# Row 128 of the sine weights: from 32 matmuls to small DMAs and a sum on VectorE

## The chip, the cores and the metric

The kernel runs on one core of a Trainium2 chip, as one program. The metric is the device time of one execution in microseconds; the median of several runs counts. The engines are named as in the profile: PE is TensorE's matmul, DVE is VectorE, ACT is ScalarE, POOL is GpSimd, and SP is SyncE, which here only issues DMAs. Each engine works through its own queue in order.

## The reference

The input is x of shape (4, 3072, 256). The kernel computes the real part of a two-dimensional discrete Fourier transform of each of the four batches, puts it through a leaky feed-forward layer, and that through a gated one with a token shift:

```python
X = np.fft.fft(np.fft.fft(x, axis=1), axis=2).real          # (4, 3072, 256)
h = X.reshape(-1, 256) @ w_in                               # (12288, 2048)
y = np.maximum(0.01 * h, h) @ w_out                         # (12288, 256)
xk = mu_k * y + (1 - mu_k) * y_prev                         # y_prev: the token before
xr = mu_r * y + (1 - mu_r) * y_prev
out = sigmoid(xr @ w_r) * (np.maximum(xk @ w_k, 0) ** 2 @ w_v)
```

## The kernel before

The transform along the sequence runs on TensorE with tables. The transform along the 256 channels is folded into the first layer's weights: a table of cosines (`cet`) and one of sines (`sot`) are multiplied with w_in once, and what comes out are cosine weights (`weh`, `wel`) and sine weights (`woh`, `wol`), each 128 rows by 2048 columns. The letters h and l stand for a high and a low part: all products are made of three matmuls, high by high, high by low and low by high. The cosine weights would have a row 128 as well, for the frequency in the middle of the 256 channels. It has no place among 128 partitions, and since the sine row of frequency 0 is zero, the values of that row are kept in row 0 of the sine weights, on partition 0.

The first layer works on tiles of 512 tokens (and their 512 mirror images). A tile has 16 units u, each of 128 of the 2048 hidden columns. For each unit `mm_a` multiplies the cosine weights, `ev_a` makes a copy of the result on DVE, and `mm_b` adds the product with the sine weights onto the same PSUM tile; `step` orders this for a unit x and the unit nx after it, and `stage_out` multiplies by w_out two units later. In `ev_a` the row's values come in: there `w128[:, u:u+1]` is a scalar per partition, so the row has to lie along the partitions, 128 values to a column of `w128`. So far `w_in_row` turned it with matmuls: 128 columns of `woh` and `wol` as weights, and a column of two numbers, (1, 0, 0, ...), as the moving operand; ACT copies what comes out into `w128`.

The weights are made while the first tile runs, in eight chunks q of 256 columns, two units each. The steps of a chunk are: `w_in_load` (SP loads 512 KB of 64-bit numbers into a buffer `st`), `w_in_parts` (ACT, DVE and POOL turn them into two 32-bit parts, f and r), `w_in_mm` (matmuls with the tables, L411 for f and L413 for r), `w_in_split` (ACT writes the high part, DVE the low part at L421) and `w_in_row`. Chunks 0 and 1 are done ahead of the loop, the others in `boot(u)`, which runs after each step of the first tile. The weights w_out go a similar way (`w_out_load`, L169 for `uol`). A load waits until its buffer is free, and the buffers are freed by POOL's multiply at L151. SP's queue is one list in program order: an issue that waits holds up those behind it. `load_c` puts one row of the sequence transform on all partitions (`cb`), for `ev_a`.

Of the kernel before, what the change touches and what calls it, by code (L numbers as in the profile page):

```python
# [78 lines left out]
def fft_mlp_kernel(ctx, tc, xs, x7, x8, x87, tb, tbs, alt, ce, so, mu, w_in, w_out, w_k, w_v, w_r, out):  # L79
# [24 lines left out]
    def act_copy(o, i):  # L104
        A.activation(o, i, ACTF.Copy)  # L105
# [277 lines left out]
    V.memset(one0[0:1].bitcast(F32), 1.0)  # L383
    V.memset(c87, 0.0)

    win, wout, wps = {}, {}, {}

    mut = misc.tile([P, 4], F32, name="mut")
    omu = misc.tile([P, 4], F32, name="omu")

    def w_in_load(q, ahead=False):
        if q < 8:
# [28 lines left out]
        V.tensor_tensor(wl2[:, :, sl], o, wh2[:, :, sl].bitcast(F32), op=ALU.subtract)  # L421


    def w_in_row(q):
        if q >= 8:
            return
        ps = win.pop(q)[0]
        for i in range(2):
            f = slice((2 * q + i) * P, (2 * q + i + 1) * P)
            o = ps[:, 2 * i:2 + 2 * i]  # L430
            T.matmul(o, woh[:, f], one0, start=True, stop=False)
            T.matmul(o, wol[:, f], one0, start=False, stop=True)
        act_copy(w128[:, 2 * q:2 * q + 2], ps[:, 0:4].rearrange("p (i t) -> p i t", t=2)[:, :, 0])

    def w_out_load(q, ahead=False):
        if q < 8:
            st = load_f64(w_out[q * 256:(q + 1) * 256].rearrange("(k p) d -> p k d", p=P), 2, D, ahead)
            s = slice(2 * q % HF, 2 * q % HF + 2)
            wout[q] = f64_hi_lo(uoh[2 * q // HF][:, s], uol[2 * q // HF][:, s], st, 2, D, *((mv, "gl") if q < 1 else (stage, "f")))
# [20 lines left out]
    def c_a(src, t0, extra):  # L460
        ps = ps_s.tile([P, 512], F32, tag="s", name="cps")
        c_mm(ps, src, t0, 0, not extra)
        if extra:
            T.matmul(ps[:4, :JP], c87[0:2], altt[0:2].bitcast(F32), start=False, stop=True)
        ev = fft.tile([4, JP], F32, tag="x7", bufs=1, name="cev") if extra else work.tile([4, JP], F32, tag="fv", bufs=2, name="cev")
        act_copy(ev, ps[:4, :JP])
        return ps, ev
# [60 lines left out]
    fold_odd(2, x0[2])  # L528
    w_in_split(1)
    w_out_load(0)  # L530
    ca = c_a(c8m, "c", False)
    c8s = c_fold()
    fold7()
    w_in_row(0)
    cs0 = c_b(c8m, "d", "o", *ca, "g")
    cur_c = load_c(0, 0)
    w_out_load(1, True)
# [2 lines left out]
    w_in_load(3)  # L540
    w_out_load(2)
    Q.dma_start(x87t, x87)
    w_in_row(1)
    po = fft_a(0, "Po")
    qo = fft_a(0, "Qo")
    for g in range(3, 6):
# [13 lines left out]
    def boot(u):  # L560
        q = u // 2
        if u == 0:
            w_in_mm(2, (1,), (0,))
            three0()
            tail0((1,))
            wout[0][1]()
            w_in_load(4)
        elif u % 2 == 0:
            w_in_row(q + 1)
            w_in_mm(q + 2)  # L570
            if q < 8:
                wout[q][0]()
            w_in_load(q + 4)
        else:
            if q == 0:
                w_in_mm(2, (1,), (1,))
            w_in_split(q + 2)
            wout[q][2]()
            w_in_parts(q + 3)
            w_out_load(q + 3)  # L580

    def mm_a(x):
# [6 lines left out]

    def ev_a(x):  # L590
        u = x["u"]
        x["ev"] = work.tile([P, W], F32, tag="as", bufs=2, name="ev")
        V.scalar_tensor_tensor(x["ev"], x["cb"], w128[:, u:u + 1], x["ps"], op0=ALU.mult, op1=ALU.add)  # L593

# [231 lines left out]
    for b in range(B):  # L826
# [4 lines left out]
        for ti in range(NT):  # L831
# [3 lines left out]
            for u in range(NF):  # L835
# [76 lines left out]
                    w2_steps.pop(0)()  # L912
                if b == B - 1:
                    if i == 33:
                        Q.dma_start(mut, mu)
                    if i == 36:
                        V.tensor_scalar(omu, mut, -1.0, 1.0, op0=ALU.mult, op1=ALU.add)
                        loaded[0] = load_tile(0)
                    if i == 39:
                        todo = do_prep(0)  # L920
                    if i in (40, 42, 44, 46):
                        todo.pop(0)()
# [219 lines left out]
```

## Time and profile before

| | us |
|---|---|
| median of three runs | 1490.4 (1489.12 to 1490.57) |
| profiled execution | 1488.97 |
| its span, first to last instruction | 1487.2 |
| PE busy | 1471.9 (99% of the span) |
| DVE, ACT, POOL busy | 1027.1, 893.2, 145.5 |

The granted TensorE clock is 1.000 over the span. A timeline row reads: start, duration, engine, line, operation, output<-inputs, shape; in brackets stands the idle time of the engine before it and what ended it. Lines are those of the kernel before; a line can be that of a helper, as L105 and L112 of the splits into high and low part.

### The profile page before, as it was taken

Reading aid. Unit: us, or ns where it says so; the run is one execution under the profiler, and the core shown is the slowest. Engines: PE = TensorE matmul, PEld = TensorE weight load, DVE = VectorE, ACT = ScalarE, POOL = GpSimd, SP = SyncE. Lnnn points to the kernel's source line nnn. Section 1 sums busy time; section 2 is a strip of 40 time slices with the busy share of each in tenths; the row PEclk is TensorE's granted clock in tenths of the full one; section 3 lists DMA queues with packets and bytes.
Section 4 is the critical chain, followed back from the end, with each engine's and each line's share of the span. In section 5 each row is a group of like instructions: output and inputs, shape, how many; then the busy total and the mean of one; then the engine's idle time right before and its main releaser. Section 6 shows DMA issues by size and latency. Waiting matters only on the chain.

```text
span 1487.2 us, 17785 instructions
## 1 busy us (share of the span) xinstructions
PE 1471.9 (99%) x6520; PEld 1209.9 (81%) x6520; DVE 1027.1 (69%) x1444; ACT 893.2 (60%) x1481; POOL 145.5 (10%) x154
## 2 busy tenths in 40 slices
PE   7999999999999999999999999999999999999998
PEld 4787888888888888888888887888888888888887
DVE  7886766766666766676767666676766666666675
ACT  5576566556666565665666656556565555555564
POOL 2444201131010221010000000000000000000000
PEclk9999999999999999999999999999999999999999
DMA  8646423564032653142220103121212212121200
GB/s 322 192 140 140 88 82 125 174 123 90 15 127 91 198 113 61 36 157 76 95 79 0 57 1 106 65 85 48 80 57 72 68 60 70 58 71 57 72 29 29
DMA packets 86396, 134.24 MB, mean 90 GB/s; under 512 B 29283, under 2 KB 49525, under 8 KB 82724
## 3 DMA queue, kind: packets, MB, share of 16 engines
q1 hardware_dynamic: 70916, 86.49, 17.9%
q0 software_dynamic: 15392, 46.61, 12.4%
q8 instruction: 51, 0.84, 0.2%
q14 instruction: 37, 0.30, 0.1%
HBM read 105.20 MB, written 27.88 MB: 89 GB/s over the span
## 4 chain that ended last, share of the span: by engine, by line
PE 91%; ACT 0%; DVE 0%; POOL 0%; DMA 0%; issue 0%; ACTq 0%; DVEq 0%
PE o L611 33%; PE v L982 17%; PE kps L939 17%; PE ps L600 8%; PE ps L588 8%; PE rps L990 4%; PE dps L632 0%; PE f2Qe L302 0%; PE f1Qe L302 0%; DMA y<-yo 0%; PE f3Qe L302 0%; PE f2Pe L302 0%; PE f1Pe L302 0%; PE f3Pe L302 0%; PE f3Po L302 0%; PE f2Qo L302 0%
## 5 line engine op out<-in xcount | busy, mean ns | idle before, releaser
L677 DVE SCALAR_TENSOR_TENSOR g<-ev,ps 128x512 f32<-128x512 f32 x192 | 131.7, 686 | 182.4 <-PE ps L600 182.4
L943 ACT ACTIVATE rl<-kps 128x512 f32<-128x512 f32 x190 | 113.7, 598 | 230.7 <-PE kps L939 227.2
L659 DVE TENSOR_TENSOR gl<-g,gh 128x1024 fp32r<-128x1024 f32 x192 | 237.8, 1239 | 1.4 <-ACT gh L105 1.4
L944 DVE SCALAR_TENSOR_TENSOR k<-kps,rl 128x512 f32<-128x512 f32 x190 | 131.5, 692 | 148.6 <-ACT rl L943 147.8
L105 ACT ACTIVATE gh<-g 128x1024 fp32r<-128x1024 f32 x192 | 202.7, 1056 | 49.4 <-PE o L611 47.9
L611 PE MATMUL o<-gh,uol 128*128 128x512 f32 x768 | 211.3, 389 | 0.5 <-DVE uol L169 0.5
L611 PE MATMUL o<-gh,uoh 128*128 128x512 f32 x768 | 211.3, 389 | 0.0
L611 PE MATMUL o<-gl,uoh 128*128 128x512 f32 x768 | 211.1, 389 | 0.0
L108 ACT ACTIVATE g<-ps 128x512 f32<-128x512 f32 x192 | 114.5, 596 | 152.4 <-DVE g L677 151.2
L611 PEld LDWEIGHTS o<-gh,uol 128*128 128x128 f32 x768 | 144.0, 188 | 30.9 <-DVE uol L169 1.1
L611 PEld LDWEIGHTS o<-gh,uoh 128*128 128x128 f32 x768 | 144.2, 188 | 30.5
L611 PEld LDWEIGHTS o<-gl,uoh 128*128 128x128 f32 x768 | 144.2, 188 | 30.0
L593 DVE SCALAR_TENSOR_TENSOR ev<-cb,w,ps 128x512 f32<-128x512 f32 x192 | 143.3, 747 | 1.9
L112 DVE TENSOR_TENSOR k2l<-k,k2h 128x512 fp32r<-128x512 f32 x190 | 129.7, 683 | 0.5 <-ACT k2h L105 0.5
L982 PE MATMUL v<-k2h,wvh 128*128 128x512 f32 x382 | 121.6, 389 | 0.1
L982 PE MATMUL v<-k2l,wvh 128*128 128x512 f32 x382 | 121.5, 389 | 0.0
L982 PE MATMUL v<-k2h,wvl 128*128 128x512 f32 x382 | 121.5, 389 | 0.0
L108 ACT ACTIVATE g<-g 128x512 f32<-128x512 f32 x192 | 119.9, 624 | 0.0
L939 PE MATMUL kps<-mh,wkh 128*128 128x512 f32 x380 | 117.2, 390 | 1.5 <-ACT mh L105 0.8
L105 ACT ACTIVATE k2h<-k 128x512 fp32r<-128x512 f32 x190 | 118.4, 623 | 0.0
L939 PE MATMUL kps<-ml,wkh 128*128 128x512 f32 x380 | 117.2, 390 | 0.1
L939 PE MATMUL kps<-mh,wkl 128*128 128x512 f32 x380 | 117.1, 389 | 0.0
(409 smaller groups left out, 2248.5 us busy)
## 6 DMA issues: line engine op xcount, KB each, us to landing
y<-yo SPq DMA_DIRECT2D x24, 512.0 KB
xa<-y SPq DMA_DIRECT2D x24, 512.0 KB
out_dram<-o SPq DMA_DIRECT2D x23, 512.0 KB
tab_a<-in_tbs POOLq DMA_DIRECT2D x8, 1158.0 KB, 6.3
tab_b<-in_tbs POOLq DMA_DIRECT2D x8, 1158.0 KB, 5.4
tab_c<-in_tbs POOLq DMA_DIRECT2D x6, 1158.0 KB, 5.4
tab_d<-in_tbs POOLq DMA_DIRECT2D x6, 1158.0 KB, 5.4
pm<-in_xs POOLq DMA_DIRECT2D x54, 128.0 KB, 3.5
```

What stands on the lines that cost most here:

```text
L105: A.activation(o, i, ACTF.Copy)
L108: A.activation(o, i, ACTF.Prelu, alpha=0.01)
L112: V.tensor_tensor(lo, src, hi.bitcast(F32), op=ALU.subtract)
L588: T.matmul(x["ps"], l[:, f], r, start=(i == 0), stop=(i == 2))
L593: V.scalar_tensor_tensor(x["ev"], x["cb"], w128[:, u:u + 1], x["ps"], op0=ALU.mult, op1=ALU.add)
L600: T.matmul(x["ps"], l[:, f], r, start=False, stop=(i == 2), skip_group_check=True)
L611: T.matmul(po[s][h], w[:, u % HF, h * P:(h + 1) * P], g[:, s], start=(u == 0 and i == 0), stop=(u == NF - 1 and i == 2))
L659: V.tensor_tensor(gl, x["g"], x["gh"].bitcast(F32), op=ALU.subtract)
L677: V.scalar_tensor_tensor(g[:, 1], x["ev"], 2.0, x["ps"], op0=ALU.mult, op1=ALU.subtract)
L939: T.matmul(ps, w[:, k, sl], x[:, k], start=(i == 0), stop=(i == 5))
L944: V.scalar_tensor_tensor(k2, ps, 0.0, r, op0=ALU.max, op1=ALU.mult)
L982: T.matmul(vps[m], w[:, f, m * P:(m + 1) * P], x, start=(f == 0 and i == 0), stop=(f == NK - 1 and i == 2))
```

## The change

`w_in_row` no longer uses TensorE. It writes the chunk's columns of row 0 of `woh` and of `wol` to a small DRAM tile (two DMAs from SP). A new function `w_in_col` reads that tile back with one DMA, 4 bytes a piece, so that the row's values lie along the partitions, high and low parts side by side; it lands in `omu` or `mut`, two small tiles that are widened for this and not needed for their own purpose until the last batch. The sum of the two parts, into `w128`, is put off to `ev_a` of the first unit that reads it (an addition on DVE). Chunks 0 and 1 are handled together, ahead of the loop; the others have their row written right after `w_in_split` and read back after `w_in_parts` of the next chunk.

```diff
--- before.py
+++ after.py
@@ -383,10 +383,10 @@
     V.memset(one0[0:1].bitcast(F32), 1.0)
     V.memset(c87, 0.0)
 
-    win, wout, wps = {}, {}, {}
-
-    mut = misc.tile([P, 4], F32, name="mut")
-    omu = misc.tile([P, 4], F32, name="omu")
+    win, wout, wps, wrd, rowsum = {}, {}, {}, {}, {}
+
+    mut = misc.tile([P, 8], F32, name="mut")
+    omu = misc.tile([P, 8], F32, name="omu")
 
     def w_in_load(q, ahead=False):
         if q < 8:
@@ -421,16 +421,18 @@
         V.tensor_tensor(wl2[:, :, sl], o, wh2[:, :, sl].bitcast(F32), op=ALU.subtract)
 
 
-    def w_in_row(q):
-        if q >= 8:
-            return
-        ps = win.pop(q)[0]
-        for i in range(2):
-            f = slice((2 * q + i) * P, (2 * q + i + 1) * P)
-            o = ps[:, 2 * i:2 + 2 * i]
-            T.matmul(o, woh[:, f], one0, start=True, stop=False)
-            T.matmul(o, wol[:, f], one0, start=False, stop=True)
-        act_copy(w128[:, 2 * q:2 * q + 2], ps[:, 0:4].rearrange("p (i t) -> p i t", t=2)[:, :, 0])
+    def w_in_row(q, n=1):
+        if q < 8:
+            f = slice(q * 256, (q + n) * 256)
+            wrd[q] = dram.tile([2, n * 256], F32, name=f"wr{q}")
+            for r, w in enumerate((woh, wol)):
+                Q.dma_start(wrd[q][r:r + 1], w[0:1, f].bitcast(F32))
+
+    def w_in_col(q, n=1):
+        if q < 8:
+            c = (omu, mut)[q % 2][:, :4 * n].rearrange("p (r u) -> p r u", r=2)
+            Q.dma_start(c, wrd[q].rearrange("r (u p) -> p r u", p=P))
+            rowsum[2 * q] = lambda: V.tensor_tensor(w128[:, 2 * q:2 * (q + n)], c[:, 0], c[:, 1], op=ALU.add)
 
     def w_out_load(q, ahead=False):
         if q < 8:
@@ -528,10 +530,11 @@
     fold_odd(2, x0[2])
     w_in_split(1)
     w_out_load(0)
+    w_in_row(0, 2)
+    w_in_col(0, 2)
     ca = c_a(c8m, "c", False)
     c8s = c_fold()
     fold7()
-    w_in_row(0)
     cs0 = c_b(c8m, "d", "o", *ca, "g")
     cur_c = load_c(0, 0)
     w_out_load(1, True)
@@ -540,7 +543,6 @@
     w_in_load(3)
     w_out_load(2)
     Q.dma_start(x87t, x87)
-    w_in_row(1)
     po = fft_a(0, "Po")
     qo = fft_a(0, "Qo")
     for g in range(3, 6):
@@ -566,7 +568,6 @@
             wout[0][1]()
             w_in_load(4)
         elif u % 2 == 0:
-            w_in_row(q + 1)
             w_in_mm(q + 2)
             if q < 8:
                 wout[q][0]()
@@ -575,8 +576,10 @@
             if q == 0:
                 w_in_mm(2, (1,), (1,))
             w_in_split(q + 2)
+            w_in_row(q + 2)
             wout[q][2]()
             w_in_parts(q + 3)
+            w_in_col(q + 2)
             w_out_load(q + 3)
 
     def mm_a(x):
@@ -589,6 +592,8 @@
 
     def ev_a(x):
         u = x["u"]
+        if (x["b"], x["t"]) == (0, 0) and u in rowsum:
+            rowsum.pop(u)()
         x["ev"] = work.tile([P, W], F32, tag="as", bufs=2, name="ev")
         V.scalar_tensor_tensor(x["ev"], x["cb"], w128[:, u:u + 1], x["ps"], op0=ALU.mult, op1=ALU.add)
 
@@ -912,9 +917,9 @@
                     w2_steps.pop(0)()
                 if b == B - 1:
                     if i == 33:
-                        Q.dma_start(mut, mu)
+                        Q.dma_start(mut[:, :4], mu)
                     if i == 36:
-                        V.tensor_scalar(omu, mut, -1.0, 1.0, op0=ALU.mult, op1=ALU.add)
+                        V.tensor_scalar(omu[:, :4], mut[:, :4], -1.0, 1.0, op0=ALU.mult, op1=ALU.add)
                         loaded[0] = load_tile(0)
                     if i == 39:
                         todo = do_prep(0)
```

On SP's queue at the start, the three DMAs of chunks 0 and 1 (`wr` is the DRAM tile, `omu` the target of the read) stand here:

```order
 L122 DMA st<-in_w_in 128x2x512
 L122 DMA st<-in_w_out 128x2x512
-L360 DMA cb_0_245<-cd_o 128x512
+L429 DMA wr_217<-wh_110 1x512
+L429 DMA wr_217<-wl_111 1x512
+L434 DMA omu<-wr_217 128x8x1
+L360 DMA cb_0_244<-cd_o 128x512
 L122 DMA st<-in_w_out 128x2x512
```

They come after the load of the first chunk of w_out and ahead of the load of `cb`. In the middle of the first tile SP's queue has these rows before the change, from the load of chunk 5 of w_out and chunk 7 of w_in on:

```order
L122 DMA st<-in_w_out 128x2x512 [waits DMAHW3_49,Pool_49]
L122 DMA st<-in_w_in 128x2x512 [waits DMAHW6_49,DMAHW0_49,Pool_49]
L122 DMA st<-in_w_out 128x2x512 [waits DMAHW5_49,Pool_49]
L360 DMA cb_1_843<-cd_o 128x256 [waits DMAHW2_49]
L360 DMA cb_1_843<-cd_e 128x256 [waits DMASW6_49]
```

and these after it, with the write and the read of chunk 5's row:

```order
L122 DMA st<-in_w_out 128x2x512 [waits Pool_49]
L122 DMA st<-in_w_in 128x2x512 [waits DMAHW7_49,Pool_49]
L429 DMA wr_758<-wh_110 1x256 [waits DMAHW5_49]
L429 DMA wr_758<-wl_111 1x256 [waits DMAHW6_49]
L434 DMA mut<-wr_758 128x4x1 [waits DMAHW6_49,DMAHW5_49]
L122 DMA st<-in_w_out 128x2x512 [waits Pool_49]
L360 DMA cb_1_837<-cd_o 128x256
L360 DMA cb_1_837<-cd_e 128x256 [waits DMAHW2_49,DMASW6_49]
```

The three DMAs stand behind the load of w_in (which waits for POOL) and ahead of the next load of w_out. On DVE, step 9 has these rows before:

```order
L143 TENSOR_SCALAR h<-fv 128x512 [waits DVE_49]
L677 SCALAR_TENSOR_TENSOR g<-ev,ps 128x512 [waits PE_49]
L593 SCALAR_TENSOR_TENSOR ev<-cb_0_245,w_86,ps 128x512 [waits PE_49]
L659 TENSOR_TENSOR gl<-g,gh 128x1024 [waits Activation_49]
L421 TENSOR_TENSOR wl_111<-wps_823,wh_110 128x2x256 [waits Activation_49]
L169 SCALAR_TENSOR_TENSOR uol_323<-r,uoh_322 128x512 [waits Pool_49]
```

and these after:

```order
L143 TENSOR_SCALAR h<-fv 128x512 [waits DVE_49]
L682 SCALAR_TENSOR_TENSOR g<-ev,ps 128x512 [waits PE_49]
L435 TENSOR_TENSOR w_86<-mut 128x2 [waits DMAHW7_49]
L598 SCALAR_TENSOR_TENSOR ev<-cb_0_244,w_86,ps 128x512 [waits DVE_49,PE_49]
L664 TENSOR_TENSOR gl<-g,gh 128x1024 [waits Activation_49]
L421 TENSOR_TENSOR wl_111<-wps_817,wh_110 128x2x256 [waits Activation_49]
L169 SCALAR_TENSOR_TENSOR uol_317<-r,uoh_316 128x512 [waits Pool_49]
```

The sum for units 10 and 11 (L435, which waits for the DMA into `mut`) now stands ahead of the `ev` of unit 10 and all that follows it. On PE the four matmuls of each chunk (L431 and L432) are gone and nothing else moved.

## Rows read from the trace of the kernel before

**Rows 1.** The page: busy time by engine; the chain that ended last, by engine.

```profile
PE 1471.9 (99%) x6520; PEld 1209.9 (81%) x6520; DVE 1027.1 (69%) x1444; ACT 893.2 (60%) x1481; POOL 145.5 (10%) x154
...
PE 91%; ACT 0%; DVE 0%; POOL 0%; DMA 0%; issue 0%; ACTq 0%; DVEq 0%
```

**Rows 2.** Busy time of PE in a window: length, busy (count), clock, DMA.

```profile
42.00:119.00 77.00, 76.75 (x364) 1.00 0.53 161
```

**Rows 3.** Busy time by window, DVE, same columns.

```profile
19.00:28.20 9.20, 8.75 (x21) 1.00 0.70 239
62.00:76.60 14.60, 13.83 (x21) 1.00 0.43 149
```

**Rows 4.** Matmuls of one line: count, ns min/median/max, first and last start, shapes.

```profile
L431 PE MATMUL wps<-one,wh x16: 166/250/271, 15.5 to 104.4; 128*128 128x2 f32 x16
```

**Rows 5.** Timeline of PE around the places that the change touches.

```profile
16.16 1.14 PE L458 MATMUL cps<-tab_c,c8m 128*4 128x386 f32 x3
...
39.46 0.17 PE L431 MATMUL wps<-one,wh 128*128 128x2 f32 x1
...
39.83 1.11 PE L411 MATMUL wps<-fv,cet 128*128 128x256 f32 x4
40.59 0.59 PE L413 MATMUL wps<-r,cer 128*128 128x256 f32 x2
...
76.78 0.43 PE L600 MATMUL ps<-Qh,wh 128*128 128x512 f32 x1
...
87.76 0.39 PE L600 MATMUL ps<-Qh,wh 128*128 128x512 f32 x1
...
92.96 0.47 PE L413 MATMUL wps<-r,cer 128*128 128x256 f32 x1
```

**Rows 6.** Timeline of ACT at the start.

```profile
15.62 0.48 ACT L105 ACTIVATE cev<-cps 4x386 f32<-4x386 f32 x1 [1.44 <-PE cps L458]
```

**Rows 7.** Timeline of DVE around units 0, 8 and 10.

```profile
28.22 0.75 DVE L593 SCALAR_TENSOR_TENSOR ev<-cb,w,ps 128x512 f32<-128x512 f32 x1
...
75.92 0.74 DVE L593 SCALAR_TENSOR_TENSOR ev<-cb,w,ps 128x512 f32<-128x512 f32 x1
...
85.54 0.74 DVE L593 SCALAR_TENSOR_TENSOR ev<-cb,w,ps 128x512 f32<-128x512 f32 x1
...
88.76 0.69 DVE L169 SCALAR_TENSOR_TENSOR uol<-r,uoh 128x512 fp32r<-128x512 f32 x1 [0.36 <-POOL r L165]
...
90.56 0.43 DVE L143 TENSOR_SCALAR h<-fv 128x512 uint32<-128x512 uint32 x1
```

**Rows 8.** Timeline of POOL.

```profile
39.13 1.29 POOL L151 TENSOR_TENSOR r<-st,h 128x512 fp32r<-128x512 f32 x1 [3.42 <-DVE c L856]
...
91.12 1.50 POOL L151 TENSOR_TENSOR r<-st,h 128x512 fp32r<-128x512 f32 x1 [2.39 <-DVE h L143]
```

**Rows 9.** Timeline of SP: start, time to issue, line, destination<-source.

```profile
23.35 0.34 SPq L360 DMA_DIRECT2D cb<-cd_o  x1
...
82.17 0.37 SPq L122 DMA_DIRECT2D st<-in_w_in  x1
...
766.88 0.45 SPq L635 DMA_DIRECT2D dc<-dcr  x1
769.86 1.48 SPq L640 DMA_DIRECT2D dct<-dc  x2
```

**Rows 10.** DMA view, 21 to 24.2 us: busy tenths in 40 slices.

```profile
DMA  9999999999999976544311000000000000000000
```

**Rows 11.** DMA view, 82.5 to 86.2 us: packets and MB; an issue, to landing.

```profile
q1 hardware_dynamic: 268, 0.52, 50.8%
...
tab_b<-in_tbs POOLq DMA_DIRECT2D x1, 1158.0 KB, 6.6
```

**Rows 12.** DMA view, 770.2 to 774.2 us: busy tenths in 40 slices.

```profile
DMA  0000000598888888988861168688699999839978
```

**Rows 13.** Tile dct: an addition of 128x16, ns min/median/max.

```profile
L645 DVE TENSOR_TENSOR dct<-dct x4: 174/175/176, 167.2 to 801.5; 128x16 f32<-128x16 f32 x4
```

## The prediction

> **What bounds the kernel now.** I read the page first. TensorE (PE) is busy for 1471.9 of 1487.2 us, and the chain that ended last is 91% PE [rows 1]. A microsecond counts only where it comes off PE's stream or holds PE up. The busy time by window says where that is so: from 42 to 119 us PE works 76.75 of 77.00 us at a granted clock of 1.00 [rows 2], so a matmul taken out there is worth its spacing, unless the next matmul waits for another engine. The same view of VectorE (DVE) names two stretches in which DVE is about as full: 8.75 of 9.20 us before 28.2, and 13.83 of 14.60 us before 76.6 [rows 3]. There PE runs at DVE's pace, and the change puts more on DVE. All of the change lies in the first 110 us. The profiled execution took 1488.97 us, 1.8 above its span and 1.4 below the median of the runs, 1490.4; I work out a difference and add it to the median. What a measurement can tell from no change is about 0.2%, or 3.0 us.
>
> **1. The matmuls that go.** Sixteen pairs, in eight groups of four between 15.5 and 104.4 us [rows 4]. In a steady group the first starts at 39.46 and what follows at 39.83 [rows 5]: 0.37 us a group, though each matmul is listed with 0.25. The two groups before 19 us are worth nothing. After the first comes the second half of c_b at 16.16 [rows 5], which accumulates onto the PSUM tile that ScalarE copies from 15.62 to 16.10 [rows 6]: the wait takes the place of the matmuls. The second lies where DVE sets the pace [rows 3]. Six groups of 0.37 leave 2.2 us at most. Not all of it stays:
> - At 39.46 PE comes soon to L413, at 40.59 [rows 5], whose operand r the multiply on POOL finishes at 39.13 + 1.29 = 40.42 [rows 8]. So 0.17 stays.
> - The group before boot(4)'s matmuls has only PE work around it: 0.37.
> - The one near 68 us is followed by mm_b of unit 8 at 76.78 [rows 5], which adds onto the PSUM tile that ev of unit 8 reads until 75.92 + 0.74 = 76.66 [rows 7]. Only 0.12 of cover, in a DVE-paced stretch: nothing stays.
> - Those near 81 and 92 us fall into the wait of point 4. The last, at 104, keeps 0.37.
>
> **2. The sums on DVE.** Seven additions (the first serves two chunks), each directly ahead of the ev that reads it. The nearest row is an addition of 128x16 at 175 ns [rows 13]; with the dependent start I take 0.2, between 0.15 and 0.25. Those of units 6 and 8 lie in the stretch before 76.6: +0.35. The others have DVE idle time behind them. The eight copies of w128 that leave ScalarE buy nothing: it is not waited for there.
>
> **3. The start.** The rows of chunks 0 and 1 go out as two writes, queued behind w_out(0); the DMA engines' shares fall to nothing at about 22.8 us [rows 10]. So the writes land at about 23.1 and SP issues the gather then, just when it would have issued cb (23.35 [rows 9]). cb is now behind the gather: its issue (two of 2048 elements took 1.48 us of SP [rows 9], so 0.4 to 0.7 for 1024) and its packets. In the trace's nearest gather, the first 2048 elements flow from about 770.9 to 772.2 [rows 12], some 1600 a microsecond, so 0.65 us here. cb is late by 0.3 to 1.3, I take 0.8. DVE's ev of unit 0 at 28.22 did not wait for cb [rows 7]; how long cb had been there no row shows. With 0.4 of slack PE loses 0.4 us, as mm_b(0) and DVE's next split stand behind that ev; with no slack and the long issue 1.3, with a full cover 0.
>
> **4. The sum that comes too late.** For a chunk q of 2 to 7 the row leaves after its split, the gather follows, and ev of unit 2q needs the sum. Between them SP has other loads. For chunk 5 the new issues stand behind the load w_in(7), which SP issues at 82.17 once a buffer is free [rows 9]. Its 0.52 MB have gone through by 86.2, beside the table that POOL asked for (tab_b, 6.6 us to landing) [rows 11]. Does a write of 1 KB wait for a load ahead of it? The nearest case: the dc row, issued at 766.88 behind two 512 KB stores, let SP go on with the gather that waits for it only at 769.86 [rows 9]: 3.0 us for 4 KB. So yes: the rows of chunk 5 land at about 86.5, not at 83. The gather then needs 1.0 us to start (769.86 to 770.9 [rows 9, 12]), 0.3 for 512 elements, and a landing, for which I take 0.4 without a row of its own; tab_b's rest shares the engines. I take 88.5, between 87.8 (no landing time) and 89.5 (as slow as the dc row, 3.0).
> DVE wants that sum at 85.54, when ev of unit 10 ran [rows 7]. It stands 3.2 us (88.5 + 0.2 - 85.54), with everything behind it: ev(10), gl(8), the split of chunk 6, uol, and the steps of w_in(7). Two of these hold PE. mm_b of unit 10, at 87.76 [rows 5], must wait for ev(10) until 89.45: 1.7 us. And the bit step at 90.56 comes 2.85 late, as the 0.36 us that DVE spent waiting for POOL at 88.76 is won back [rows 7]; POOL's multiply for w_in(7), which ended at 91.12 + 1.50 = 92.62 [rows 8], then ends at 95.5, and PE's L413 at 92.96 [rows 5] waits for it: 2.55 us. The larger of the two counts: +2.55, with bounds of 1.85 and 3.55 from those of the landing. It already holds the two groups of matmuls near 81 and 92.
> The other chunks are in time by the same steps. Closest is chunk 4, whose gather lands at about 75 against 75.92 [rows 7].
>
> **Sum.** +0.40 (start) - 0.17 - 0.37 + 0.35 (two sums) + 2.55 - 0.37 = +2.4 us: 1492.8 us. The ends of the terms together give +1.2 to +4.4; as they are hardly met at once, this case's own range is 1491.8 to 1494.3.
>
> **Rivals.**
> - *The rows do not queue behind the load.* Their writes go out when issued, at 82.6 and 82.9 after the load's issue; with a gather of 1.7 us the sum is there for ev(10) if they land by 83.8. Against it is the dc row's 3.0 us [rows 9], for it that those stores write the same memory, while the load ahead here reads it. Then point 4 is gone and its two groups count: +0.40 - 0.17 - 0.37 + 0.35 - 0.12 - 3 x 0.37 = -1.0: 1489.4. With the start covered as well, -1.4; the floor is the 2.2 of point 1, 1488.2. This change cannot make the kernel faster by over 0.2% in any case I can work out. Chance 0.23.
>   The Trainium skill, page DMA: Bandwidth & Descriptors, section Anatomy of one DMA, gives a DMA a fixed cost of about 2.0 us, most of it the confirmation that the write has landed. By that alone, an estimate, write and gather take 4.0 us from 82.9, the sum starts at 86.9 instead of 85.54, and PE would lose about 0.9 at L413 and end near 1491. The dc row took longer than that.
> - *The start costs more.* cb comes over 1.0 us later than DVE can bear, since the gather's issue takes the 1.48 us of SP that a pair took [rows 9] and its packets move while cb's wait. Then the first term is 1.5 in place of 0.4: +3.5, 1493.9, slower by more than 0.2%; it decides once cb is 1.4 us late without slack. For it: SP and the queue serve in order. Against: the gather has half the elements of one of those two. Chance 0.22.
> - Late gathers at several chunks, or one that moves at a tenth of the rate: over 1495. Chance 0.05.
>
> **The numbers.** The first case has 0.50. It ends over 1493.4 in about a quarter of its cases (0.13), the second rival in most (0.17), the last in all: slower 0.35. Faster needs under 1487.4, below every floor: 0.05 for what I have not seen. Same 0.60. The range that leaves 2 in 10 out cuts the lower half of the first rival and the upper end of the second: 1489.0 to 1495.0.
>
> **What would show it.** Right: on DVE the sum ahead of ev(10) waits over 2 us for a DMA, the others next to none; POOL's multiply for w_in(7) and PE's L413 follow it late; PE's mm_b of unit 0, which waits for ev(0), comes 0 to 1 us later; after 105 us the two traces run with a fixed offset. Wrong: the sum of unit 10 waits for nothing (the first rival), or DVE's longest new wait is ahead of ev(0) (the second). If PE's lead at 60 us is not about 0.1 us, point 1 is mis-sized.

## The result and the profile after

The changed kernel takes **1506.4 us** (median of 5 runs, 1504.5 to 1509.9) against 1489.1 of the kernel before on the same chip (5 runs, 1489.1 to 1490.6): a ratio of 1.0115, 95% interval 1.0104 to 1.0127. It is slower by 17.3 us, where the prediction had 1492.8 us (1489.0 to 1495.0). The profiled execution of the changed kernel took 1509.9 us, the longest of the five; its span is 1508.1 us, 20.9 above that of before. So its trace shows some 3.5 us more loss than the median has.

The page of the changed kernel, busy time and the chain by engine, beside [rows 1]:

```profile
PE 1476.5 (98%) x6488; PEld 1210.1 (80%) x6488; DVE 1029.6 (68%) x1451; ACT 892.5 (59%) x1473; POOL 142.8 (9%) x154
...
PE 92%; DVE 3%; DMA 2%; issue 1%; ACT 1%; POOL 0%; SPq 0%; DVEq 0%; ACTq 0%; POOLq 0%
```

PE has 32 matmuls fewer and yet 4.6 us more busy time, and DMAs, which had no share of the chain, now have 2% of it. The busy time by window says where (window, its length; PE's busy time and count, those of weight loads, DVE, ACT, POOL; granted clock, DMA share, GB/s):

```profile
42.00:119.00 77.00, 62.57 (x266) 48.41 (x265) 51.56 (x78) 36.70 (x63) 23.49 (x20) 0.91 0.49 134
47.00:57.00 10.00, 1.72 (x8) 0.37 (x6) 0.86 (x3) 1.62 (x3) 0.00 (x0) 0.79 1.03 200
57.00:64.00 7.00, 6.89 (x18) 5.48 (x19) 6.90 (x12) 2.27 (x4) 1.30 (x1) 0.56 0.09 11
...
105.00:108.00 3.00, 3.00 (x10) 2.35 (x8) 2.93 (x6) 0.00 (x0) 0.00 (x0) 0.59 0.20 67
141.00:145.00 4.00, 4.00 (x13) 3.09 (x12) 2.57 (x3) 1.12 (x2) 0.85 (x1) 0.58 0.75 122
```

In the stretch in which PE had been busy for 76.75 of 77.00 us [rows 2], it works 62.57. From 47 to 57 us nearly nothing runs on any engine while the DMA engines are full (1.03): everything waits for a transfer. And the granted clock, 1.00 before, is near 0.5 (1.2 of 2.4 GHz) for most of three short stretches, the first two directly behind such a standstill.

The timeline of DVE names what is waited for: L435 is the new sum, L598 the ev behind it, and the bracket is DVE's idle time ahead of an instruction with what ended it. It answers to [rows 7]:

```profile
28.23 0.16 DVE L435 TENSOR_TENSOR w<-omu 128x4 f32<-128x4 f32 x1
...
56.03 0.16 DVE L435 TENSOR_TENSOR w<-omu 128x2 f32<-128x2 f32 x1 [11.84 <-DMA omu<-wr]
56.30 0.75 DVE L598 SCALAR_TENSOR_TENSOR ev<-cb,w,ps 128x512 f32<-128x512 f32 x1
73.45 0.15 DVE L435 TENSOR_TENSOR w<-mut 128x2 f32<-128x2 f32 x1
...
88.06 0.16 DVE L435 TENSOR_TENSOR w<-omu 128x2 f32<-128x2 f32 x1 [1.05 <-DMA omu<-wr]
...
103.35 0.16 DVE L435 TENSOR_TENSOR w<-mut 128x2 f32<-128x2 f32 x1 [5.38 <-DMA mut<-wr]
```

Three gathers are late: that of chunk 2 (unit 4) by 11.8 us, of chunk 4 (unit 8) by 1.05, of chunk 5 (unit 10) by 5.4. The other sums wait for no gather. The timeline of PE, beside [rows 5]; L605 is mm_b, L616 the output matmuls:

```profile
57.10 0.80 PE L605 MATMUL ps<-Qh,wh 128*128 128x512 f32 x1 [8.39 <-DVE ev L598]
...
63.19 1.09 PE L616 MATMUL o<-gl,uoh 128*128 128x512 f32 x4
...
89.13 0.50 PE L605 MATMUL ps<-Qh,wh 128*128 128x512 f32 x1 [1.16 <-DVE ev L598]
...
104.42 0.79 PE L605 MATMUL ps<-Qh,wh 128*128 128x512 f32 x1 [4.10 <-DVE ev L598]
```

From the start of mm_b of each unit in both traces, the changed kernel is behind by 0.27 us at unit 0, 0.02 at unit 3, 8.48 at unit 4 (57.10 against 48.62), 10.83 at unit 5, 10.37 at unit 7, 12.35 at unit 8, 16.67 at unit 10 (104.42 against 87.76 [rows 5]), 17.78 at unit 11, 18.25 at unit 16, 20.31 at unit 17, and 20.25 from there to 884 us. So the loss comes in steps: the three waits, and a step directly behind each long one that is no wait. From mm_b's first matmul to the last group of output matmuls of that step PE took 6.09 us at unit 4 (57.10 to 63.19) and 3.31 before (48.62 to 51.93), because it ran at half clock: 2.8 us on top of the 8.4. The last step, at unit 17, is also half clock (the last window above). The same places of PE before, L600 for mm_b and L611 for the output matmuls:

```profile
48.62 0.50 PE L600 MATMUL ps<-Qh,wh 128*128 128x512 f32 x1
...
51.93 1.07 PE L611 MATMUL o<-gl,uoh 128*128 128x512 f32 x4
```

**Why the gathers are late** stands on SP's timeline (start, time to issue, line, destination and source), beside [rows 9]:

```profile
37.11 0.22 SPq L429 DMA_DIRECT2D wr<-wl  x1
43.52 0.38 SPq L434 DMA_DIRECT2D omu<-wr  x1
...
62.37 0.37 SPq L122 DMA_DIRECT2D st<-in_w_in  x1
...
63.17 0.24 SPq L429 DMA_DIRECT2D wr<-wl  x1
66.37 0.38 SPq L434 DMA_DIRECT2D mut<-wr  x1
...
94.58 0.37 SPq L122 DMA_DIRECT2D st<-in_w_in  x1
...
95.37 0.25 SPq L429 DMA_DIRECT2D wr<-wl  x1
101.14 0.38 SPq L434 DMA_DIRECT2D mut<-wr  x1
```

A gather leaves when its row has landed. With a 512 KB load ahead on SP and nothing else, the row of chunk 3 needs 3.2 us (63.17 to 66.37). With POOL's table in the DMA engines as well, that of chunk 5 needs 5.8. The DMA view from 94.5 to 101.5 us has the table that POOL issued at 94.50 (the last number: us from issue to landing); the row had landed by 101.14, 0.3 us before it:

```profile
tab_b<-in_tbs POOLq DMA_DIRECT2D x1, 1158.0 KB, 6.9
```

For chunk 2 the chain that ended last has the same and a worse thing (start, length, what):

```profile
37.11 6.34 DMA wr<-wl
...
43.52 12.48 DMA omu<-wr
```

The gather of 512 pieces takes 12.5 us here; that of chunk 5, as large, takes 2.2 (101.14 to 103.33). The difference is what POOL had issued just ahead, by its timeline; the table at 35.34, on its way for 7.9 us, is what the row met:

```profile
35.34 0.60 POOL L195 DMA_DIRECT2D tab_a<-in_tbs  x1
...
40.60 0.58 POOL L195 DMA_DIRECT2D tab_b<-in_tbs  x1
41.18 2.66 POOL L231 DMA_DIRECT2D pm<-in_xs  x2
```

And the DMA view of 43 to 57 us, by queue (q0 is POOL's, q1 SP's; packets, MB, share of the 16 engines):

```profile
q0 software_dynamic: 921, 2.55, 84.6%
q1 hardware_dynamic: 800, 0.53, 15.6%
```

POOL's queue has 84.6% of the engines in that stretch, most of it for the two accumulating transfers into pm (L231, 768 KB each). The kernel before has them as well; there nothing small that an engine waited for had to get through beside them:

```profile
40.38 0.58 POOL L195 DMA_DIRECT2D tab_b<-in_tbs  x1
40.96 2.66 POOL L231 DMA_DIRECT2D pm<-in_xs  x2
```

### The profile page after: what moved, and what is told of

The parts are those of the page before. It is cut to its first block, busy times and chain, and to the rows that moved or that the text cites. A ratio compares the mean times of both kernels' runs of the same rounds, so it can differ in the third digit from the quotient of the medians.

```text
span 1508.1 us, 17761 instructions
## 1 busy us (share of the span) xinstructions
PE 1476.5 (98%) x6488; PEld 1210.1 (80%) x6488; DVE 1029.6 (68%) x1451; ACT 892.5 (59%) x1473; POOL 142.8 (9%) x154
## 4 chain that ended last, share of the span: by engine, by line
PE 92%; DVE 3%; DMA 2%; issue 1%; ACT 1%; POOL 0%; SPq 0%; DVEq 0%; ACTq 0%; POOLq 0%
PE o L616 33%; PE v L987 17%; PE kps L944 17%; PE ps L605 8%; PE ps L591 8%; PE rps L995 4%; DMA omu<-wr 1%; DMA wr<-wl 1%; PE wps L411 1%; DVE gl L664 1%; PE dps L637 0%; DVE ev L598 0%; PE cps L460 0%; DVE g L682 0%; DMA st<-in_w_in 0%
## 5 line engine op out<-in xcount | busy, mean ns | idle before, releaser
L616 PE MATMUL o<-gh,uol 128*128 128x512 f32 x768 | 212.8, 392 | 0.6 <-DVE uol L169 0.5
L616 PE MATMUL o<-gh,uoh 128*128 128x512 f32 x768 | 213.2, 392 | 0.0
L616 PE MATMUL o<-gl,uoh 128*128 128x512 f32 x768 | 211.1, 389 | 0.0
L616 PEld LDWEIGHTS o<-gh,uol 128*128 128x128 f32 x768 | 145.1, 189 | 31.9 <-DVE uol L169 1.6
L616 PEld LDWEIGHTS o<-gh,uoh 128*128 128x128 f32 x768 | 145.6, 190 | 31.0
L616 PEld LDWEIGHTS o<-gl,uoh 128*128 128x128 f32 x768 | 144.3, 188 | 30.1
L598 DVE SCALAR_TENSOR_TENSOR ev<-cb,w,ps 128x512 f32<-128x512 f32 x192 | 143.4, 747 | 2.7 <-PE ps L591 0.2
```

Source lines behind the costliest of these rows:

```text
L616: T.matmul(po[s][h], w[:, u % HF, h * P:(h + 1) * P], g[:, s], start=(u == 0 and i == 0), stop=(u == NF - 1 and i == 2))
```

## Experiments

Three theories for late rows and gathers stood against each other. Theory 1: POOL's bulk transfers on the DMA engines that all queues share. Theory 2, the prediction's: the order on SP's queue, behind a load. Theory 3: 512 pieces of 4 bytes are slow by themselves; the 2.2 us of chunk 5 speak against it. There is no result for a variant without the stop in DRAM (each part of the row straight onto the partitions), so what that stop costs is not measured. Times below are medians with the ratio to the kernel before, run on the same chip (1489.0 to 1489.4 us each time).

**All waits gone.** The sums from unit 4 on are left out, the transfers stay.

```diff
+    V.memset(w128, 0.0)
...
-        if (x["b"], x["t"]) == (0, 0) and u in rowsum:
+        if (x["b"], x["t"]) == (0, 0) and u == 0:
```

> Leaves out the six sums on DVE from unit 4 on: row 128 of the sine weights counts as zero there. The 32 matmuls are gone as in the changed kernel, and all writes and gathers still move. If the loss comes only through the sums that wait for their gathers, this kernel ends at the time of before plus 0.3 (start) minus 0.4 (matmuls of steady groups that PE keeps) minus up to 0.7: 1488 to 1490 us, PE has no wait over 0.5 us at L605 for ev, and the granted clock stays at 1.00 from 42 to 119 us. If the new transfers harm by themselves (they make the split weights, the tables or the folds of others late), it stays over 1495 us, with PE waiting at L411, L413 or L591 instead.

Measured: 1489.2 us, ratio 1.0001 (0.9992 to 1.0010), clock 1.00. The whole loss comes through the sums; the transfers harm nobody else. It also shows what there was to win. PE is ahead by 0.5 us at unit 8, 0.9 at unit 12 and 1.4 at unit 13, gives 0.6 back between units 14 and 17 and the last 0.7 at about 900 us. With every sum from unit 4 on gone, and every wait for a gather with it, nothing that can be measured is won.

**POOL's two accumulations later.**

```diff
-                if b == 0 and i == 1:
+                if b == 0 and i == 2:
                     even0(0, 1)
                     even0(1, 1)
+                if b == 0 and i == 1:
                     V.tensor_tensor(c87[0:1], x87t[:, 0], x87t[:, 1], op=ALU.add)
```

> Issues the two accumulating transfers into pm on POOL's queue one step later, so that they are not in the DMA queues at 41 to 56 us; nothing is left out. Theory 1 (the gather of chunk 2 takes turns with POOL's transfers on the same DMA engines): that gather lands at about 47 to 49 in place of 56.0 us, the sum of unit 4 waits under 2 us in place of 11.8, PE's 8.4 us ahead of mm_b of unit 4 go, and with them the half clock of 52.7 to 63 us: 10 to 12 us less than the changed kernel, 1494 to 1497 us; what chunks 4 and 5 lose stays. Theory 2 (order on SP's queue) and theory 3 (512 pieces of 4 bytes are slow by themselves): the gather takes its 12 us as before, and the time stays at 1504 to 1510 us.

Measured: 1500.7 us, ratio 1.0074 (1.0057 to 1.0090). The chain now reads:

```profile
37.16 4.55 DMA wr<-wl
...
41.78 4.91 DMA omu<-wr
...
46.72 2.07 DVE w L435
```

The gather takes 4.9 us in place of 12.5, PE loses 0.99 us at unit 4 in place of 8.46, and there is no half clock behind it. Theory 1 holds for chunk 2: most of what was lost there came from pm's transfers beside the gather. The sum of unit 10 still waits for 5.3 us. The time is 5.7 us less, not 10 to 12 as forecast; in part since the profile from which it was forecast was the longest of its runs: at the same place, unchanged, the sum of unit 4 waited 7.2 us in the table experiment below, not 11.8. New in the rows is a sum of 128x2 that takes 2.07 us; see below.

**Rows on another queue.**

```diff
-                Q.dma_start(wrd[q][r:r + 1], w[0:1, f].bitcast(F32))
+                (A if q else Q).dma_start(wrd[q][r:r + 1], w[0:1, f].bitcast(F32))
```

> The row writes of chunks 2 to 7 are issued by ScalarE instead of SyncE, directly behind ScalarE's own work on the split weights; the gathers stay on SyncE. Theory 2, the prediction's (the row of chunk 5 stands behind the load w_in(7) on SP's queue): on another queue the row lands within 2 us of its issue, the gather of chunk 5 is issued at 97 to 98 us in place of 101.1, the sum of unit 10 waits under 1.5 us in place of 5.4, and 4 to 6 us come back: 1501 to 1503 us; unit 4 keeps its wait. Theory 1 (rows land when POOL's table load has gone through the DMA engines that all queues share): the rows of chunks 2, 4 and 5 land where they did, at about 43.4, 85.9 and 101.1 us, whatever queue they are in, and the time is that of the changed kernel within 3 us.

Measured: 1502.1 us (1496.6 to 1503.3), ratio 1.0077 (1.0058 to 1.0096). The rows of chunk 5 leave at 84.4 and 85.4 us, and the gather follows directly behind the load w_in(7), at 90.14. Then the gather itself stands behind load and table: the sum waits 3.35 us, at 96.42. The rows had thus landed by then. They had left 4 us before table and load were issued (89.60 and 89.68), so chunk 5 is a test of neither theory: the run moved the loss from the row to the gather. The time lies in the range of theory 2, but the sum's wait, forecast at under 1.5 us, does not. Chunk 2 tells more: its row, on ScalarE's queue, still took 4.6 us (37.65 to 42.21) with POOL's table in the DMA engines. Another queue alone does not make it quick.

**The table one step later.**

```diff
-                    if i in (k_u, k_u + lag):
+                    if i in ((k_u + 1, k_u + lag + 1) if (b, i < 15) == (0, True) else (k_u, k_u + lag)):
```

> POOL's table loads of the first pass are issued one step later, so that they don't leave with the row writes of chunks 4 and 5; the order on SyncE is that of the changed kernel, and nothing is left out. Theory 1: the rows of chunks 4 and 5 take 3.2 us to their gather's issue, as chunk 3's do in the changed kernel (a load ahead on SP, no table), in place of 5.3 and 5.8; the sum of unit 8 waits for nothing and that of unit 10 for 2.5 to 3.5 in place of 5.4 us; 3 to 5 us come back: 1501 to 1503 us. Theory 2: they take 5.3 and 5.8 us as before, and the time stays within 2 us of the changed kernel's, unit 4's wait being as long.

Measured: 1500.7 us (1495.1 to 1503.0), ratio 1.0070 (1.0043 to 1.0098). SP's timeline at chunk 5:

```profile
88.57 0.37 SPq L122 DMA_DIRECT2D st<-in_w_in  x1
...
89.36 0.25 SPq L429 DMA_DIRECT2D wr<-wl  x1
92.56 0.38 SPq L434 DMA_DIRECT2D mut<-wr  x1
```

And DVE's:

```profile
94.69 0.16 DVE L435 TENSOR_TENSOR w<-mut 128x2 f32<-128x2 f32 x1 [2.74 <-DMA mut<-wr]
```

With the load ahead and no table the row takes 3.2 us, exactly as chunk 3's, and the sum waits 2.7 in place of 5.4; that of unit 8 waits for nothing. Half of chunk 5's lateness is the table (theory 1). The other half is SP's order (theory 2); how much of that half is the load's transfer and how much SP's wait ahead of it, this run does not split.

**SP's load behind row and gather.**

```diff
-            w_in_load(q + 4)
...
             w_in_col(q + 2)
+            w_in_load(q + 4)
```

> On SyncE the load of the next columns of the sine and cosine weights goes behind the two row writes and the gather of the same step, in place of ahead of them; nothing is left out. For chunk 5 the low half of the split is there at 90.8 us in the changed kernel's trace, but the row writes leave at 95.0 and 95.4, behind a load that waited for its buffer until 94.6. Theory 2 (order on SP's queue, the wait for the buffer included): the rows of chunks 4 and 5 leave when their split is done, their gathers are issued within 2 us of that (as those of chunk 6 are, 1.2 us after the row, with no load ahead), the sums of units 8 and 10 wait for nothing, and 7 to 9 us come back: 1496 to 1500 us, with unit 4's wait as it is or shorter. Theory 1 (POOL's transfers alone): the rows still land only when POOL's table has landed, the sum of unit 10 still waits over 3 us, and the time is over 1502 us.

Measured: 1495.4 us (1493.2 to 1496.9), ratio 1.0038 (1.0023 to 1.0052). SP at chunk 5:

```profile
80.23 0.24 SPq L429 DMA_DIRECT2D wr<-wl  x1
81.38 0.38 SPq L434 DMA_DIRECT2D mut<-wr  x1
83.98 0.40 SPq L122 DMA_DIRECT2D st<-in_w_in  x1
```

The row lands 1.15 us after its issue, the gather is gone before load and table come, and the sums of units 8 and 10 wait for nothing: PE's offset is 1.74 at unit 8 and 1.80 at unit 10. The row leaves before the table too (83.90), so this run alone does not split load from table. It also shows a third part of the lateness: in the changed kernel SP stood at the load until its buffer was free (94.58), while the split of chunk 5 had ended at 90.8. Unit 4's sum waits 3.5 us here.

**Both moves together.** The edits of the last experiment and of POOL's accumulations.

> Both moves together: the two accumulating transfers of POOL one step later, and SyncE's loads behind rows and gather; nothing is left out. If POOL's transfers at chunk 2 and SP's order at chunks 4 and 5 are all that makes the sums late, no sum waits over 1 us, PE has no wait over 1 us for ev, and the time is that of the kernel without the sums, 1489 to 1490.5 us: no faster than before. If a part of the lateness has another cause, it stays over 1492 us and the trace shows the wait that is left.

Measured: 1493.8 us (1491.7 to 1495.1), ratio 1.0028 (1.0019 to 1.0037). No sum waits over 0.94 us, PE's offset at unit 10 is 0.37, and still the kernel is 4.5 us above before. So late gathers were not all. The offset grows to 1.93 at unit 16 and, at half clock, to 3.92 at unit 17, while the sums of units 10, 12 and 14, with nothing to wait for, take 0.96, 1.05 and 0.69 us in place of 0.16.

**Another form of the sum.**

```diff
-            rowsum[2 * q] = lambda: V.tensor_tensor(w128[:, 2 * q:2 * (q + n)], c[:, 0], c[:, 1], op=ALU.add)
+            rowsum[2 * q] = lambda: V.scalar_tensor_tensor(w128[:, 2 * q:2 * (q + n)], c[:, 0], 1.0, c[:, 1], op0=ALU.mult, op1=ALU.add)
```

> The kernel with both moves (POOL's two transfers later, SyncE's loads behind row and gather), and each sum written as scalar_tensor_tensor (times 1.0, plus) in place of tensor_tensor; nothing is left out. In the trace of the kernel with both moves no sum waits over 1 us for a gather, yet it ends 4.4 us above the kernel without sums: its sums of units 10, 12 and 14 take 0.96, 1.05 and 0.69 us in place of 0.16 and end within 0.03 us of the end of POOL's multiply into r (86.78, 99.51, 110.88). Theory A (a tensor_tensor on SBUF operands is held while POOL multiplies, and this one form is): the new form is not held, takes about 0.2 us everywhere, DVE gets 2.1 us back in the stretch from unit 10 to 14, and the time falls to 1489.5 to 1492 us. Theory B (any DVE instruction that reads two operands from SBUF is held): the sums are as long as before, and the time stays within 1 us of 1493.8. The half clock at unit 17 (2 us) comes or not with the execution in either case.

Measured: 1493.2 us (1491.4 to 1495.3), ratio 1.0024 (1.0015 to 1.0033). The form makes no difference; DVE's timeline at unit 10:

```profile
85.48 0.96 DVE L435 SCALAR_TENSOR_TENSOR w<-mut 128x2 f32<-128x2 f32 x1
```

And POOL's:

```profile
85.10 1.32 POOL L151 TENSOR_TENSOR r<-st,h 128x512 f32<-128x512 f32 x1 [2.43 <-issue]
```

The sum ends at 86.44 and POOL's multiply at 86.42. It came out as theory B says: either form, reading two operands from SBUF, is held to the end of POOL's multiply where that began first. An instruction with one operand in SBUF and one in PSUM is not: in the kernel before, ev of unit 10 takes 0.74 us at 85.54 [rows 7], all of it beside POOL's multiply from 85.18 to 86.48. The Trainium skill, page GPSIMD Engine Reference, section Specifications, says that GpSimd shares its SBUF interfaces with VectorE and that instructions with two SBUF inputs contend for them; both forms here agree.

**Three chunks by matmuls.** Chunks 2, 4 and 5 as before, 0, 1, 3, 6 and 7 by small DMAs.

```diff
+            if q + 1 in MM:
+                w_in_row_mm(q + 1)
             w_in_mm(q + 2)
...
-            w_in_row(q + 2)
+            if q + 2 not in MM:
+                w_in_row(q + 2)
...
-            w_in_col(q + 2)
+            if q + 2 not in MM:
+                w_in_col(q + 2)
```

> The changed kernel with the rows of chunks 2, 4 and 5 turned by matmuls as in the kernel before, and those of 0, 1, 3, 6 and 7 by small DMAs; nothing is left out. If the late sums of units 4, 8 and 10 are all that the change costs beyond its prediction, no sum waits over 0.5 us for a gather and the time is that of the kernel before within 2 us: plus 0.3 to 0.6 at the start, minus 0.37 for chunk 6, plus up to 1.4 where the sums of units 12 and 14 are held by POOL's multiply: 1489.5 to 1491 us. If the other chunks' gathers or the start cost more than the trace of the changed kernel shows, it stays over 1492 us.

Measured: 1491.05 us (1490.6 to 1492.4), ratio 1.0013 (1.0004 to 1.0022). No sum waits for a gather. PE is ahead by 0.29 us at unit 12, behind by 1.04 at unit 16 and by 1.53 from unit 17 on: the held sums of units 12 and 14 (1.05 and 0.68 us) take more than the matmuls of five chunks gave.

**The sum on ScalarE.** The kernel with both moves, with the low half added as a bias.

```diff
-            rowsum[2 * q] = lambda: V.tensor_tensor(w128[:, 2 * q:2 * (q + n)], c[:, 0], c[:, 1], op=ALU.add)
+            def add():
+                for j in range(2 * n):
+                    A.activation(w128[:, 2 * q + j:2 * q + j + 1], c[:, 0, j:j + 1], ACTF.Prelu, bias=c[:, 1, j:j + 1], alpha=1.0)
+            rowsum[2 * q] = add
```

> The kernel with both moves, its sums taken off DVE: ScalarE adds the low half as a per-partition bias, one activation of 128x1 for each column, at the same place in the program; nothing is left out. Both forms of the sum on DVE were held to the end of POOL's multiply (0.96, 1.05 and 0.68 us). If that hold is what is left of the loss between units 8 and 15 (the two held sums of units 12 and 14 cost 1.3 us of PE in the kernel with three chunks on matmuls, from -0.29 to +1.04), no sum takes over 0.3 us here, PE's offset against the kernel before stays between -1 and 0.5 us up to unit 16, and the time is 1489.5 to 1491.5 us. If ScalarE is late by it (it waits for the gather ahead of its copy of gh), or what is left has another cause, the time stays within 1 us of 1493.8.

Measured: 1492.2 us (1490.7 to 1493.9), ratio 1.0020 (1.0011 to 1.0029). The sums take 0.46 us for two columns and none is held; PE's offset stays between -0.6 and 0.3 up to unit 16, as forecast. Then unit 17 adds 2.1 us at half clock (PE's clock is 0.62 from 122 to 126 us), and the time is above the range that I gave. The best version with all rows by DMA is thus still 3 us behind the kernel before.

**The sums alone.** The kernel before, matmuls and all, with seven additions on a tile of its own, and then on tiles that the kernel has.

```diff
+    dum = misc.tile([P, 8], F32, name="dum")
...
+        if (x["b"], x["t"]) == (0, 0) and u in (0, 4, 6, 8, 10, 12, 14):
+            V.tensor_tensor(dum[:, 0:2], dum[:, 2:4], dum[:, 4:6], op=ALU.add)
```

> The kernel before, matmuls and all, with an addition of 128x2 on DVE ahead of ev of units 0, 4, 6, 8, 10, 12 and 14, on a small tile that nothing else uses: the sums alone, with no transfer and nothing to wait for. By the prediction's price (0.2 us each, two of them in a stretch that DVE paces) it costs 0.35 us: 1489.2 to 1490 us. If additions that meet POOL's multiply are held to its end, those of units 10, 12 and 14 take 0.7 to 1.1 us, PE loses 1.0 to 2.3 us between units 8 and 15, and the time is 1490.3 to 1492 us.

Measured: 1509.4 us (1508.2 to 1510.6), ratio 1.0134 (1.0118 to 1.0149): far outside both forecasts. PE is 4.9 us behind at 884 us, and 16.7 more come after 900 us, where no such addition runs. So the second run, on the tiles mut and omu:

```diff
+    V.memset(mut, 0.0)
...
+            V.tensor_tensor(omu[:, 0:2], mut[:, 0:2], mut[:, 2:4], op=ALU.add)
```

> The kernel before with the same seven additions as in the run with the small tile of its own, but on the two small tiles that the kernel has anyway, so that no address moves; nothing else is changed. In the run with the tile of its own PE was 4.9 us behind at 884 us, of which 1.9 came between units 10 and 16 and 2.1 at unit 17, and some 17 us more came after 900 us, where the matmuls into v and kps took 395 ns in place of 389 and 390. If the tile's 32 bytes cause the later part (all tiles behind it lie elsewhere), those matmuls take 389 and 390 ns again and the time is that of the kernel before plus what the additions cost: by the hold of POOL's multiply 1.5 to 2.5 us, 1490.5 to 1492 us; by the prediction's price for the sums 0.35 us, 1489.3 to 1489.8 us. If the additions themselves bring the later part about, the time stays over 1505 us.

Measured: 1492.9 us (1491.3 to 1493.7), ratio 1.0021 (1.0012 to 1.0030). DVE's timeline at unit 12:

```profile
98.28 1.05 DVE L594 TENSOR_TENSOR omu<-mut 128x2 f32<-128x2 f32 x1
...
99.91 2.33 DVE L662 TENSOR_TENSOR gl<-g,gh 128x1024 fp32r<-128x1024 f32 x1
```

And POOL's:

```profile
98.00 1.31 POOL L151 TENSOR_TENSOR r<-st,h 128x512 f32<-128x512 f32 x1 [4.68 <-ACT uoh L164]
...
99.85 1.30 POOL L165 TENSOR_TENSOR r<-r,fv 128x512 f32<-128x512 f32 x1
```

Seven additions that take 0.15 us each when alone, with no transfer and nothing to wait for, cost this kernel 3.7 us. Each of those at units 10, 12 and 14 is held to the end of POOL's first multiply (at unit 12, 98.28 + 1.05 = 99.33 against 98.00 + 1.31 = 99.31). So is that at unit 4, for 1.10 us, but PE loses nothing there. By that delay gl, which took 1.39 us in the kernel before, meets POOL's second multiply and takes 2.33. PE's offset goes from 0.03 at unit 10 to 0.64, 1.21 and 1.83 behind these three, and then by 2.05 at unit 17, where the clock falls to 0.77 (122 to 126 us) and 0.81 (126 to 130). More than half of the 3.7 us is thus half clock. In the kernel before the same place has waits of 1.34 and 0.30 us, and the clock stayed at 1.00 in the profiled execution.

**The clock.** The changed kernel, with PE kept at work through its first long wait by multiplying with zeros.

```diff
+    zer = misc.tile([P, P], F32R, name="zer")
...
+        if (x["b"], x["t"], u) == (0, 0, 4):
+            for _ in range(28):
+                T.matmul(state["po"][0][0], zer, qh, start=False, stop=False, skip_group_check=True)
```

> The changed kernel with 28 matmuls of 128x512 by a matrix of zeros, accumulated onto a running output sum directly ahead of mm_b of unit 4, where PE waits; the result is the same. At 0.23 us each they fill 6.4 us of a wait that was 8.4 us in the profiled run. If the half clock from 52.7 to 63.0 us comes from PE's standing still, and costs 2.8 us (the 18 matmuls after the wait took 6.1 us from the first to the last start, 3.3 in the kernel before), then the clock stays at 1.00 up to 64 us here, those 18 take 3.3 us, and the time is 2 to 3 us less: 1503 to 1505 us. If the clock falls for another reason, it falls as before and the time is that of the changed kernel, or up to 6 us more where the wait of a run is shorter than the filling.

Measured: 1503.2 us (1503.0 to 1504.1), ratio 1.0092 (1.0077 to 1.0107), 3.2 us less than the changed kernel. PE at unit 4 (L610 is mm_b, L621 the output matmuls):

```profile
48.84 6.78 PE L608 MATMUL o<-Qh,zer 128*128 128x512 f32 x28
55.46 0.40 PE L610 MATMUL ps<-Qh,wh 128*128 128x512 f32 x1
...
58.68 1.08 PE L621 MATMUL o<-gl,uoh 128*128 128x512 f32 x4
```

The sum waited for 7.6 us here and was there at 52.0, so the filling held PE some 2.4 us longer than the wait would have (ev ended at 53.05, mm_b starts at 55.46). The clock stayed at 1.00, and the same matmuls take 3.22 us in place of 6.09. PE's standing still is what brings the half clock there, and its price is the 2.8 us that the traces gave. The trace has no half clock at unit 17 either, so the 3.2 us between the medians are not this place alone.

## Why the prediction was wrong

**The step that failed** is the sentence of point 4 that the other chunks are in time by the same steps, chunk 4 being the closest. The chunk that costs most is chunk 2, which I had not worked out: 8.4 us of wait and 2.4 of half clock (the 2.8 less the matmuls that are gone there), 10.8 of the 20.9 us in the trace. The steps of point 4 know SP's queue and a load ahead in it. At chunk 2 it is POOL's queue that fills the DMA engines: a table beside the row, then a table and two accumulations beside the gather, which the trace of before shows at 40 us as much as that of after. I looked at POOL's transfers at one chunk only, the one where SP's order had pointed to.

- **1, the matmuls that go:** right. PE gains 0.25 us to unit 3 (0.17 forecast) and 0.44 per steady group (0.37 forecast) in the run without sums, loses the gain near 68 us again at unit 8, as forecast, and keeps none of it at the end.
- **2, the sums on DVE:** mis-sized, and in the wrong place. 0.2 us each was the price of an addition alone. The two that I charged, at units 6 and 8, cost PE nothing in the run of the sums alone (its offset stays within 0.05 us up to unit 10). Of those that I put at nothing, four are held by POOL's multiply, 0.7 to 1.1 us; the three at units 10, 12 and 14 also push gl into the next one. The term of +0.35 measured +1.8 between units 10 and 16, and 3.7 us in the time, with the half clock at unit 17. The trace of before had such a hold: a DVE instruction on 128x384 elements (L286) takes 1.72 us at 59.23, just after POOL's multiply of 59.22 to 60.53 began, and 0.56 at 90.90, ahead of one.
- **3, the start:** right. PE is 0.27 us behind at unit 0 (0.40 forecast), and 0.2 to 0.9 in the other profiled runs with this start.
- **4, the sum that comes too late:** right in its mechanism and place, wrong in size. The sum of unit 10 waits 5.4 us, not 3.2, and PE is held by ev(10), not by POOL's multiply for w_in(7). I took 3.6 us for the row behind the load (82.9 to 86.5); a load alone makes it 3.2, the table beside it 5.8. The gather's 2.0 us were right (2.2). PE loses 4.3 there, not 2.55, and 1.1 of half clock behind it.
- **No term for the clock.** The kernel before runs at 1.00 throughout the stretch [rows 2], and I priced each wait as a wait. A wait of 8.4 us cost 10.8, one of 4.1 cost 5.4.

The first rival, rows that don't queue behind the load, is refuted by chunk 3's 3.2 us and by the run with the load behind. The section of the Trainium skill named there has its 2.0 us from transfers that GpSimd issues. SyncE's row with nothing ahead took 1.15 us here, the quickest gathers 2.1 to 2.2. The second rival, a dearer start, did not happen. What happened is the last one, late gathers at several chunks, to which I gave 0.05; nothing in my working excluded it but that sentence.

The ledger of the profiled execution, by PE's offset: 0.3 start, 10.8 chunk 2, 2.0 chunk 4 (with 0.5 of regained matmul time lost again), 5.4 chunk 5, 0.9 from unit 13 to 16 (the sums of units 12 and 14 take 0.47 and 0.68 us), 2.1 half clock at unit 17, 0.6 behind 884 us, less 1.1 that the matmuls gave.

**What is not settled:** why the clock falls at unit 17 in some profiled runs (the changed kernel, both moves, the sums alone) and not in others (the other form of the sum, three chunks by matmuls) with the same two waits of 1.34 and 0.8 us; and how far the lateness of chunk 2 spreads between executions, of which the profiles give only 7.2 to 11.8 us.

## What to carry to other kernels

A transfer of 2 KB that an engine waits for can be as slow as what is in the DMA engines when it gets there, on whatever queue that stands (2.2 to 12.5 us here): draw the bulk transfers of all queues on one time axis, and do it for every repetition of the new transfer, not for the one that looks closest. Issue the small one ahead of the bulk, and ahead of any issue that must first wait for a buffer. Price a small VectorE instruction by what GpSimd does at its place, and a wait of TensorE by the clock behind it.

## What was not expected of the hardware

- **A row of 1 KB lands with the bulk transfer beside it.** Rows took 1.15 us alone, 3.2 behind a 512 KB load, 5.8 with a table of 1158 KB on POOL's queue as well, and that one landed within 0.3 us of the table. The Trainium skill, page DMA: Bandwidth & Descriptors, section Queues, rings and completion order, says that a completion's increment lands only after every earlier write of that DMA engine, across its queues. These rows agree; no run here takes a single DMA engine apart.
- **The same gather of 512 pieces** took 2.2 us and 12.5 us, by what POOL had queued.
- **A DVE addition of two elements a partition** took 0.15 or up to 2.07 us; it ended with POOL's multiply, where that had begun first.
- **A new tile of 32 bytes a partition** came with 16.7 us more behind 900 us. With the tile of its own the matmuls of the second half took longer. The group of one line's matmuls (count, busy time, mean ns of one, idle time) with that tile:

```profile
L986 PE MATMUL v<-k2h,wvh 128*128 128x512 f32 x382 | 124.0, 395 | 0.0
```

And without it:

```profile
L985 PE MATMUL v<-k2h,wvh 128*128 128x512 f32 x382 | 121.6, 389 | 0.1
```

The instructions are the same but for the tile, which moves the tiles behind it. That the address is what matters was not tried by itself, and the cause stays open: a tile of 512 bytes (the zeros of the clock experiment) left these matmuls at 389, and so did the changed kernel, in which mut and omu are wider by 16 bytes each.
